# The first expert of a routed feed-forward moved from plain fp32 matmuls to split fp32r matmuls, with the order of the program remade

## The chip, the cores and the metric

The kernel runs on one core of a Trainium2 chip. The metric is the device time of one execution in microseconds (us). The engines of the core are PE (TensorE, matmuls; PEld is its weight load), DVE (VectorE), ACT (ScalarE), POOL (GpSimd) and SP (SyncE, which here issues nearly all transfers). Each engine takes its instructions in the order in which the program lists them.

## The reference

Attention with four sink positions and a window of 128 comes first; its output, as 3072 tokens of 512 numbers, goes through a layer of 8 experts, of which each token uses one:

```python
scores = np.where(is_sink | in_window, q @ k.T / sqrt(64), -1e9)   # 4 x 8 heads, 768 x 768
a = softmax(scores)
x = (a @ v) as 3072 x 512
e_idx = np.argmax(x @ w_gate, axis=1)
for e in range(8):
    mask = e_idx == e
    h = np.maximum(x[mask] @ w1[e], 0.0)            # 512 -> 1024
    out[mask] = gate_w * eom * (h @ w2[e])          # 1024 -> 512
```

Everything is float32.

## The kernel before

**Attention** runs over 16 pairs of heads (4 batches of 4 pairs). For a pair, PE computes the scores in three steps (L1256) into tiles named d, DVE masks them and takes row maxima (L1270, L1272; the "fold"), ACT takes exponentials (L1277, two for each of 6 blocks of 128 rows) into e, PE transposes them (L1305), ACT copies them out (L1308), POOL masks two copies f and g (L384), PE multiplies by v (L1373) and adds the sinks (L1396), ACT copies the result to ot (L1402, with a small tick before the second half, L1387), PE computes the gate logits (L1412) and transposes the output (L1445), and DVE scales both (lw, L1420; x, L1448) before SP stores x to a table xd in device memory.

**Routing** follows after each batch, as some thirty small DVE instructions and three matmul steps (L524 to L622): which expert each token takes, its place in the expert's list (pos, tokpos, ohrow), and after the second and third batch which experts have most tokens (u, gt, rank, perm, order).

**Experts.** A slot is a piece of one expert: up to 6 units of 64 tokens with the whole 4 MB of that expert's weights. Four slots of 256 tokens, numbers 0 to 3, are early: two for the experts ranked after the second batch, two after the third. Thirteen more follow when all tokens are routed, over sizes of 384, 256, 128 and 64 tokens. For a slot, POOL gathers the tokens (xg, L899), PE transposes them (L964), ACT and DVE write them as high and low parts xh and xl (L967, L969); eight tiles of 512 KB are loaded to raw (L936), ACT writes each as its high part (L939, names ending in h, such as wa0h) and DVE the rest as its low part (L943, names ending in l). The products go as three matmuls, high by high, low by high and high by low (L1083 for the first layer, L1122 for the second); the first layer's result is split into hh and hl as well (L1000, L1003).

**The plain slot.** `PLAIN = 1` makes slot 0 an exception. Its eight weight tiles are loaded as plain float32, without conversion, into the space of four pairs wa0 to wa3 (the h and l tile of a pair hold one weight tile each), and it multiplies in plain fp32 (L1064 and L1122), where each matmul stands as two records in the trace. Its result needs no low part (hh alone, L1070).

**Buffers.** Raw has four tiles. Weights have four pairs wa from the start, three pairs wb which take the space of q, k and e once attention has read those for the last time (`close_q`), and six pairs wc which take the rest of the attention's space (`close_a`). The low parts hl and xl lie in a pool mp that also opens with `close_q`.

**Order.** The order of all instructions is set by a planner (`Plan.order`) from a model of costs, from offsets for each kind of step (`AT`), and from times pinned to single steps (`PIN`). The `SOFT` slack lets the plain slot's matmuls give way to attention. Loads before the end of attention are paced by small writes of POOL to their target (`touch`, L1143), each behind a mask step of a certain pair.

Of the kernel before, what the change touches and what calls it, by code (L numbers as in the profile page):

```python
# [51 lines left out]
SOFT = 10509  # L52
SLOT0, STEP, PLAIN, FSTEP = 186561, 20000, 1, 800
# [4 lines left out]
    "load": -31160, "v": -31097, "vs": -28707, "s0": -1104, "s1": 2946, "s2": 3862, "fold": 6328, "exp": -295,  # L58
    "tr0": 5205, "tr1": 8027, "tr2": 9541, "trc": 0, "mask": -3518, "guard": 127, "pack": 3756, "skT": 10500,
# [297 lines left out]
def moe_kernel(tc, qT, kx, vx, vs, wgo, w1, w2, nsink, window, out):  # L357
# [7 lines left out]
    with ctx:  # L365
        const = ctx.enter_context(tc.tile_pool(name="const", bufs=1))
        rt = ctx.enter_context(tc.tile_pool(name="rt", bufs=1))
# [538 lines left out]
        def weights(p, k, which, reg, whole, at, plain=False):  # L906
# [3 lines left out]
            for i in range(4):  # L910
# [19 lines left out]
                if k == PLAIN and not which:  # L930
                    touch([raw], lambda raw=raw: p.get(raw), paced[11 + (8 + i) // 3, (8 + i) % 3], at + i)
# [796 lines left out]
```

## Time and profile before

| | |
|---|---|
| time, median of 3 runs | 514.47 us (514.12 to 519.23) |
| the profiled execution | 515.66 us |
| its span in the trace | 514.0 us |
| PE busy | 480.6 us (94%) |
| DVE, ACT, POOL busy | 326.8, 281.6, 159.3 us |
| moved by DMA | 112.35 MB, mean 219 GB/s |

The profiled execution is one run beside the three; 1.7 us of its time lie outside its span. Busy time of PE is an upper view of its work, because the ends of its matmuls are modelled and overlap.

### The profile page before, as it was taken

The numbers are of one execution on the slowest core, as the hardware profiler recorded it, in microseconds if no ns is written. First come the engines' busy times: TensorE is split into PE (matmuls) and PEld (weight loads), VectorE is DVE, ScalarE is ACT, GpSimd is POOL, SyncE is SP. The second block draws the span as 40 slices with busy tenths as digits, with TensorE's granted clock in tenths as the row PEclk, the third lists the DMA queues.
The fourth block names the chain that finished last, engine by engine and source line by source line (L and its number), as shares of the span: only waits on it lengthen the run. The fifth ranks groups of instructions, "written<-read, shape, count | busy, mean of one in ns | idle before, by whom it ended". The sixth has DMA issues, their size and how long they took to land.

```text
span 514.0 us, 14382 instructions
## 1 busy us (share of the span) xinstructions
PE 480.6 (94%) x5625; PEld 390.4 (76%) x5625; DVE 326.8 (64%) x702; ACT 281.6 (55%) x774; POOL 159.3 (31%) x284
## 2 busy tenths in 40 slices
PE   7899988979899979999999999999999999999993
PEld 3677867757678866688898988978975977986861
DVE  5575866888686667559998963237525688267710
ACT  3878885657597534454556334246525667257510
POOL 5536543647653530204082113022203210101011
PEclk9999999979999999999999999999999999999998
DMA  6674664536695293856498753819679978888930
GB/s 203 214 224 111 220 217 126 169 100 195 200 346 178 87 297 94 282 176 204 153 307 319 233 205 96 294 46 339 199 275 332 331 270 284 301 297 320 352 121 29
DMA packets 61295, 112.35 MB, mean 219 GB/s; under 512 B 8027, under 2 KB 27617, under 8 KB 61218
## 3 DMA queue, kind: packets, MB, share of 16 engines
q1 hardware_dynamic: 56578, 97.06, 56.8%
q0 software_dynamic: 4352, 13.87, 7.5%
q8 instruction: 47, 0.77, 0.6%
q10 hardware_dynamic: 288, 0.41, 0.3%
q14 instruction: 30, 0.25, 0.2%
HBM read 98.14 MB, written 13.31 MB: 217 GB/s over the span
## 4 chain that ended last, share of the span: by engine, by line
PE 62%; DVE 13%; DMA 8%; ACT 6%; issue 6%; POOL 1%; another core or an unknown queue 1%; SPq 1%; POOLq 0%; DVEq 0%; ACTq 0%
PE d L1122 21%; PE d L1083 15%; DMA raw<-in_w_dram 5%; PE d L1373 5%; PE d L1256 4%; PE d L1096 3%; PE d L1064 3%; PE tp L1305 2%; ACT e L1277 2%; DVE nmx L1272 2%; PE tp L964 2%; PE tp L1445 2%; DVE d L1270 2%; PE d L1412 2%; PE d L1030 1%
## 5 line engine op out<-in xcount | busy, mean ns | idle before, releaser
L1277 ACT ACTIVATE e<-d,nmx 128x132 f32<-128x132 f32 x192 | 68.8, 369 | 1.4
L982 POOL DMA_INDIRECT out_dram<-y,idx x20 | 21.2, 1058 | 136.8 <-ACT y L979 107.8
L1000 ACT ACTIVATE hh<-d 128x512 fp32r<-128x512 f32 (+1 forms) x32 | 20.7, 649 | 58.4 <-PE d L1083 56.6
L1256 PE MATMUL d<-k,q 64*64 64x196 f32 (+3 forms) x1088 | 44.2, 283 | 6.8 <-DVE lw L1420 2.0
L1256 PEld LDWEIGHTS d<-k,q 64*64 64x64 f32 x1088 | 36.8, 134 | 15.1 <-issue 6.1
L1003 DVE SCALAR_TENSOR_TENSOR hl<-d,hh 128x512 fp32r<-128x512 f32 (+1 forms) x32 | 24.0, 753 | 34.6 <-ACT hh L1000 34.3
L899 POOL DMA_INDIRECT xg<-xd,idx x20 | 24.5, 1224 | 67.3 <-PE tp L964 44.3
L1373 PE MATMUL d<-f,v 64*64 64x64 f32 (+1 forms) x768 | 41.3, 252 | 2.0 <-ACT e L1277 1.2
L1373 PE MATMUL d<-g,v 64*64 64x128 f32 (+1 forms) x640 | 38.9, 253 | 3.8 <-ACT tick L1387 2.3
L384 POOL TENSOR_SCALAR_AFFINE_SELECT g<-f 128x512 f32<-128x512 f32 (+1 forms) x48 | 27.7, 577 | 43.7 <-ACT f L1308 41.7
L1277 ACT ACTIVATION_READ_ACCUMULATOR e<-d,nmx 128x1 f32 x192 | 39.1, 203 | 0.0
L1373 PEld LDWEIGHTS d<-f,v 64*64 64x64 f32 x768 | 34.1, 135 | 5.9 <-issue 2.5
L1270 DVE COPY_PREDICATED d<-maskf,d 128x512 f32<-128x512 int32 (+1 forms) x48 | 29.0, 604 | 14.0 <-PE d L1256 8.9
L1272 DVE TENSOR_REDUCE nmx<-d 128x4 f32<-128x528 f32 x48 | 33.9, 707 | 1.7
L979 ACT ACTIVATE y<-d,sc 128x512 f32<-128x512 f32 (+1 forms) x28 | 17.5, 656 | 30.6 <-PE d L1122 21.4
L1373 PEld LDWEIGHTS d<-g,v 64*64 64x64 f32 x640 | 29.8, 134 | 5.6 <-ACT tick L1387 3.1
L1305 PE MATMUL tp<-ident,e 128*128 128x128 f32 x192 | 30.3, 285 | 2.4 <-DVE x L1448 1.3
L1308 ACT COPY f<-tp 128x512 f32<-128x512 f32 x48 | 27.5, 586 | 6.6 <-PE tp L1305 6.4
L1305 PEld LDWEIGHTS tp<-ident,e 128*128 128x128 f32 x192 | 21.3, 143 | 10.4 <-DVE x L1448 2.3
L384 POOL TENSOR_SCALAR_AFFINE_SELECT f<-f 128x512 f32<-128x512 f32 (+1 forms) x48 | 27.0, 563 | 3.3
L982 POOL DMA_INDIRECT out_dram<-y,idx_e x8 | 11.8, 1480 | 51.4 <-ACT y L979 49.9
L1284 ACT ACTIVATE nmx<-nmx 128x4 f32<-128x4 f32 x48 | 10.0, 209 | 26.9 <-DVE nmx L1272 26.6
(481 smaller groups left out, 1447.8 us busy)
## 6 DMA issues: line engine op xcount, KB each, us to landing
raw<-in_w_dram SPq DMA_DIRECT2D x96, 512.0 KB
v<-in_vx_dram SPq DMA_DIRECT2D x8, 768.0 KB
xd<-x SPq DMA_DIRECT2D x16, 384.0 KB
k<-in_kx_dram SPq DMA_DIRECT2D x15, 396.0 KB
q<-in_qT_dram SPq DMA_DIRECT2D x15, 384.0 KB
wa1h<-in_w_dram SPq DMA_DIRECT2D x3, 512.0 KB
wa1l<-in_w_dram SPq DMA_DIRECT2D x3, 512.0 KB
wa2h<-in_w_dram SPq DMA_DIRECT2D x3, 512.0 KB
```

What stands on the lines that cost most here:

```text
L384: nc.gpsimd.affine_select(out=ap, in_=ap if src is None else src, pattern=pattern, compare_op=op, fill=fill, base=base, channel_multiplier=cm)
L899: nc.gpsimd.indirect_dma_start(out=p.get(key), out_offset=None, in_=xd[0:n + 1, :], in_offset=bass.IndirectOffsetOnAxis(ap=ids(), axis=0))
L982: nc.gpsimd.indirect_dma_start(out=where, out_offset=bass.IndirectOffsetOnAxis(ap=ids(), axis=0), in_=p.get(yk)[:, 0:m], in_offset=None, b ...
L1083: nc.tensor.matmul(out=p.get(ps)[:, j, 0:cols], lhsT=a, rhs=p.get(x)[:, d, 0:cols], start=d == 0 and i == 0, stop=d == ND - 1 and i == 2)
L1122: nc.tensor.matmul(out=p.get(ys[s][0])[:, ys[s][1], :], lhsT=h[a][:, s * P:(s + 1) * P], rhs=w[b_], start=f == 0 and i == 0, stop=f == NF ...
L1256: nc.tensor.matmul(out=to, lhsT=get(q)[r, qs], rhs=get(k)[r, c:c + n], start=True, stop=True)
L1270: nc.vector.copy_predicated(out=y[:, :, D + 4:3 * D + 4].rearrange("p n (u c) -> p n u c", u=2), mask=bc(maski[:, 1, 4:CW].rearrange("p (u ...
L1272: nc.vector.tensor_reduce(out=top(), in_=z[:, :, :, D:3 * D + 4], axis=AX.X, op=ALU.max, negate=True)
L1277: nc.scalar.activation(out=get(e)[:, t, a, :], in_=by_step()[:, a, i, D:3 * D + 4], func=AF.Exp, bias=get(nmx)[:, a, t:t + 1], scale=SCALE ...
L1305: nc.tensor.transpose(out=get(tp)[:, i, :], in_=get(e)[:, 2 * j + i // 2, i % 2, 4:CW], identity=ident)
L1308: nc.scalar.copy(out=get(f)[:, two].rearrange("p t a r -> p (t a) r"), in_=get(tp))
L1373: nc.tensor.matmul(out=o, lhsT=get(v)[rows_, kt, p % 2 * P + a * D:p % 2 * P + (a + 1) * D], rhs=get((f, g)[src == "g"])[rows_, kt, a, c0: ...
```

## The change

`PLAIN` becomes 0. Slot 0 then runs like slots 1 to 3: its weights go through raw and through a high and a low part, its products are three fp32r matmuls in place of one plain fp32 matmul, and its hidden values get a low part. Since this starts while attention still holds q, k and e, the low parts hl (4 tiles) and xl move from the pool mp, which is gone, to the pool m0, which is open from the start. The four pairs wa now hold half of slot 0's weights, and the other half waits in raw for `close_q`. All numbers that set the order (`AT`, `PIN`, `SLOT0`, `SOFT`) are new; `SOFT` no longer applies to any step.

```diff
-SOFT = 10509
-SLOT0, STEP, PLAIN, FSTEP = 186561, 20000, 1, 800
+SOFT = 9763
+SLOT0, STEP, PLAIN, FSTEP = 184276, 20000, 0, 800
...
-    "load": -31160, "v": -31097, "vs": -28707, "s0": -1104, "s1": 2946, "s2": 3862, "fold": 6328, "exp": -295,
+    "load": -23906, "v": -17027, "vs": -32208, "s0": -211, "s1": 21366, "s2": 9120, "fold": 12815, "exp": -634,
...
-                    touch([raw], lambda raw=raw: p.get(raw), paced[11 + (8 + i) // 3, (8 + i) % 3], at + i)
+                    touch([raw], lambda raw=raw: p.get(raw), paced[11 + (8 * PLAIN + i) // 3, (8 * PLAIN + i) % 3], at + i)
...
-                             ("hh", 4, "m0")):
+                             ("hh", 4, "m0"), ("hl", 4, "m0"), ("xl", 1, "m0")):
...
-            opened["mp"] = mctx.enter_context(tc.tile_pool(name="mp", bufs=1, side="right", reuse_waits="tile"))
...
-        for fam, n, pool, gate, n0 in (("hl", 4, "mp", xq, 0), ("xl", 1, "mp", xq, 0), ("hr", 3, "mc", xa, 0), ("xf", 1, "mc", xa, 0),
+        for fam, n, pool, gate, n0 in (("hr", 3, "mc", xa, 0), ("xf", 1, "mc", xa, 0),
```

In the new program every line after the tables stands 15 lines further down: the fold is L1285 and L1287, the casts L954, the gate L1427, and so on.

The first place is DVE in the routing of the second batch, up to the first lw that stands behind it; d is a score tile, and L1270/L1272 are folds. Before:

```order
L671 TENSOR_TENSOR perm<-rank,io_95 128x16
L672 TENSOR_TENSOR pe<-perm,io_95 128x16
L584 SCALAR_TENSOR_TENSOR den<-z,den 128x6
L585 RECIPROCAL denw<-den 128x96
L675 TENSOR_REDUCE od<-pe 128x2
L676 CAST order_i<-od 128x2
L1420 TENSOR_TENSOR lw_2240<-d_118,rs_1729 128x192
```

The same place on DVE in the new order:

```order
L681 TENSOR_REDUCE rank<-gt 128x8
L1285 COPY_PREDICATED d_119<-maskf,d_119 128x4x128
L1287 TENSOR_REDUCE nmx_2159<-d_119 128x2x2
L686 TENSOR_TENSOR perm<-rank,io_95 128x16
L687 TENSOR_TENSOR pe<-perm,io_95 128x16
L608 CAST jf<-ji 128x12
L609 TENSOR_TENSOR ohj<-jf,ioj 128x96
L690 TENSOR_REDUCE od<-pe 128x2
L691 CAST order_i<-od 128x2
L615 TENSOR_TENSOR ohrow<-io_97,jf 128x768
L1285 COPY_PREDICATED d_118<-maskf,d_118 128x4x128
L1287 TENSOR_REDUCE nmx_2240<-d_118 128x2x2
```

Before, nineteen rows (174 to 192 of DVE, nearly all of routing) stand between two folds; now folds stand after the rank step and after ohrow, with twelve rows ahead of the first and seven between the two.

The second place is ACT among the exponentials of the thirteenth and fourteenth pair (L1277 before, L1292 after). Before:

```order
L1277 ACTIVATE e_2592,rs_2593<-d_120,nmx_2534 128x132 x4
L1387 COPY tick_2785<-d_118 128x1
L1284 ACTIVATE nmx_2754<-nmx_2754 128x2x2
L1277 ACTIVATE e_2800,rs_2801<-d_119,nmx_2754 128x132 x4
L1308 COPY f_2724<-tp_2788 128x512
```

The same place on ACT in the new order:

```order
L1292 ACTIVATE e_2609,rs_2610<-d_118,nmx_2563 128x132 x4
L1402 COPY tick_2778<-d_119 128x1
L954 CAST wa1h<-raw_2627 128x1024
L1299 ACTIVATE nmx_2749<-nmx_2749 128x2x2
L954 CAST wa2h<-raw_2654 128x1024
L1323 COPY f_2702<-tp_2789 128x512
L1292 ACTIVATE e_2831,rs_2832<-d_120,nmx_2749 128x132 x2
L1417 COPY ot_2853<-d_119 128x2x3x128
L1292 ACTIVATE e_2831,rs_2832<-d_120,nmx_2749 128x132 x2
L1323 COPY f_2702<-tp_2855 128x512
L954 CAST wa3h<-raw_2768 128x1024
```

Three of the four casts of slot 0's first-layer weights now stand between exponentials (the first stands 14 rows ahead of the second); before, ACT's first cast came after attention's last exponential.

The third place is PE at the end of attention, from the sinks of the last pair on. Before, a first-layer step of slot 1 (L1083, 24 matmuls) stood between the sinks and the gate, and slot 0's second layer began behind the gate:

```order
L1396 MATMUL d_119<-psk_194,vst_195 64x384 x4
L1083 MATMUL d_118<-xh_3657,wb0h 128x256
...
L1445 MATMUL tp_3765<-ident,ot_3759 128x128 x4
L1445 MATMUL tp_3770<-ident,ot_3759 128x128 x2
L1412 MATMUL d_119<-wgt,ot_3759 64x16 x24
L1122 MATMUL d_120<-wa2h,hh_3453 128x512 x4
```

The same place on PE in the new order:

```order
L1411 MATMUL d_118<-psk_194,vst_195 64x384 x4
L1427 MATMUL d_118<-wgt,ot_3795 64x16 x24
L1460 MATMUL tp_3829<-ident,ot_3795 128x128 x4
L1460 MATMUL tp_3837<-ident,ot_3795 128x128 x2
L1137 MATMUL d_119<-wb0h,hh_3583 128x512
L1137 MATMUL d_119<-wb0l,hh_3583 128x512
```

The gate now stands right behind the sinks of its pair, and slot 0's second layer reads its weights from wb0 in high and low parts.

## Rows read from the trace of the kernel before

**Rows 1.** The page: busy time and share of the engines; PE clock in 40 slices.
```profile
PE 480.6 (94%) x5625; PEld 390.4 (76%) x5625; DVE 326.8 (64%) x702; ACT 281.6 (55%) x774; POOL 159.3 (31%) x284
PEclk9999999979999999999999999999999999999998
```

**Rows 2.** The chain that ended last, 155 to 262 us: start, length, piece.
```profile
162.92 1.73 PE d L1064 x8
...
170.11 5.18 PE d L1064 x24
...
196.60 7.06 PE d L1122 x16
203.67 2.88 PE d L1083 x24
206.55 6.87 PE d L1122 x16
213.41 2.88 PE d L1083 x24
216.29 8.16 PE d L1122 x36
```

**Rows 3.** Instructions of L1064: durations min/median/max in ns, first and last start.
```profile
L1064 PE MATMUL d<-xh,wa0h x16: 379/379/483, 162.8 to 181.5; 128*128 128x256 f32 x16
```

**Rows 4.** Groups of instructions by line on ACT and DVE.
```profile
L939 ACT CAST wa0h<-raw 128x1024 fp32r<-128x1024 f32 x11 | 11.5, 1048 | 9.6 <-PE d L1096 8.5 <-DMA raw<-in_w_dram 0.6 <-issue 0.3
...
L1003 DVE SCALAR_TENSOR_TENSOR hl<-d,hh 128x512 fp32r<-128x512 f32 (+1 forms) x32 | 24.0, 753 | 34.6 <-ACT hh L1000 34.3
...
L969 DVE TENSOR_TENSOR xl<-tp,xh 128x512 fp32r<-128x512 f32 x22 | 14.7, 683 | 8.9 <-ACT xh L967 8.9
L943 DVE TENSOR_TENSOR wa0l<-raw,wa0h 128x1024 fp32r<-128x1024 f32 x11 | 13.4, 1218 | 1.9 <-ACT wa0h L939 1.7
```

**Rows 5.** Busy time in windows of 20 us (PE, PEld, DVE, ACT, POOL), clock, DMA share, GB/s.
```profile
140.00:160.00 20.00, 19.19 (x509) 15.79 (x509) 16.48 (x39) 15.99 (x73) 8.80 (x27) 1.00 1.00 322
160.00:180.00 20.00, 20.00 (x231) 17.31 (x227) 13.03 (x34) 11.75 (x33) 11.21 (x20) 1.00 0.27 88
180.00:200.00 20.00, 17.12 (x288) 12.90 (x279) 12.38 (x40) 6.22 (x14) 4.50 (x4) 1.00 0.69 227
200.00:220.00 20.00, 20.00 (x91) 13.52 (x90) 12.48 (x13) 11.73 (x14) 3.07 (x2) 1.00 0.71 223
220.00:240.00 20.00, 19.90 (x142) 18.13 (x141) 15.78 (x35) 10.88 (x15) 4.19 (x4) 1.00 0.64 199
```

**Rows 6.** Windows of 2 us around the routing of the second batch.
```profile
104.00:106.00 2.00, 1.09 (x20) 0.71 (x20) 1.86 (x10) 1.41 (x7) 0.76 (x1) 1.00 0.08 21
106.00:108.00 2.00, 0.41 (x7) 0.42 (x10) 1.90 (x8) 0.00 (x0) 0.39 (x2) 0.90 0.00 0
108.00:110.00 2.00, 1.85 (x26) 1.30 (x18) 1.93 (x5) 0.02 (x1) 1.22 (x2) 0.50 0.23 25
110.00:112.00 2.00, 1.40 (x7) 1.21 (x8) 1.97 (x4) 1.90 (x10) 0.00 (x0) 0.50 0.86 276
112.00:114.00 2.00, 2.00 (x29) 1.47 (x29) 1.09 (x6) 1.31 (x6) 0.81 (x2) 0.50 0.98 318
114.00:116.00 2.00, 2.00 (x58) 1.72 (x52) 1.00 (x3) 1.35 (x6) 1.70 (x2) 0.89 0.01 2
sum 12.00, PE 8.75 PEld 6.83 DVE 9.74 ACT 5.99 POOL 4.89; mean PE 1.46 PEld 1.14 DVE 1.62 ACT 1.00 POOL 0.81
```

**Rows 7.** PE's timeline there: start, length, what, and the idle time before it.
```profile
107.59 1.65 PE L1256 MATMUL d<-k,q 64*64 64x128 f32 x24 [2.03 <-DVE lw L1420]
```

**Rows 8.** PE's waits over the whole run, the longest.
```profile
PE d L1373 <- ACT tick L1387: 2.3, 2, 2.1
```

**Rows 9.** Window of 226 to 250 us; then PE's timeline in it.
```profile
226.00:250.00 24.00, 22.56 (x164) 20.22 (x164) 22.53 (x69) 13.01 (x19) 5.48 (x5) 1.00 0.56 173
...
248.63 0.66 PE L964 MATMUL tp<-ident,xg 128*128 128x128 f32 x4 [1.01 <-DVE tab L622]
```

**Rows 10.** The chain, 376 to 400 us: a load of raw behind four others.
```profile
379.67 0.38 SPq L925
...
383.90 9.27 DMA raw<-in_w_dram
```

More of the change, by code (lines that the diff above doesn't have):

```diff
@@ L51 @@
 PAIR, RAT = 9500, 17500
-SOFT = 10509
-SLOT0, STEP, PLAIN, FSTEP = 186561, 20000, 1, 800
+SOFT = 9763
+SLOT0, STEP, PLAIN, FSTEP = 184276, 20000, 0, 800
 AT = {
-    "load": -31160, "v": -31097, "vs": -28707, "s0": -1104, "s1": 2946, "s2": 3862, "fold": 6328, "exp": -295,
-    "tr0": 5205, "tr1": 8027, "tr2": 9541, "trc": 0, "mask": -3518, "guard": 127, "pack": 3756, "skT": 10500,
[3 rows of a table removed]
+    "load": -23906, "v": -17027, "vs": -32208, "s0": -211, "s1": 21366, "s2": 9120, "fold": 12815, "exp": -634,
+    "tr0": 2554, "tr1": 8112, "tr2": 11988, "trc": -937, "mask": 20086, "guard": -5960, "pack": 2664, "skT": 10478,
[3 rows of a table added]
 }
 PIN = {
[59 rows of a table removed]
[74 rows of a table added]
 }
@@ L1672, in moe_kernel @@
                 now = tensors(Now())
-                for fam, n, pool, n0 in (("sc", 8, "mx", 0), ("xg", 2, "mc", 4), ("xh", 1, "mx", 0), ("xl", 1, "mp", 0), ("hh", 4, "m0", 0), ("hl", 4, "mp", 0),
+                for fam, n, pool, n0 in (("sc", 8, "mx", 0), ("xg", 2, "mc", 4), ("xh", 1, "mx", 0), ("xl", 1, "m0", 0), ("hh", 4, "m0", 0), ("hl", 4, "m0", 0),
                                          ("hr", 3, "mc", 0), ("y", 4, "mc", 0), ("raw", RAW, "stg", 0)):
```

139 rows, old and new, of tables (AT, PIN) are left out of this document.

## The prediction

> **What bounds the kernel now.** I read first the busy shares of the page [rows 1]: PE is busy 94% of the span, the next engine 64%, so only PE's work and PE's few gaps can pay. I then read the chain that ended last around the place where slot 0 runs [rows 2]. The reader is to see that from 162.9 us on nearly every piece of the chain is a PE piece, so that a matmul saved there moves all that follows. Windows of 20 us show the same from the other side [rows 5]: from 140 to 240 us PE is busy 96.2 of 100 us. DVE and ACT have room there, and DMA (share 0.27 to 1.00) is not full except before 160 us. Last I looked where PE loses time inside attention. The windows of 2 us from 104 to 116 us [rows 6] are the worst stretch: PE is busy 8.75 of 12 us, and its granted clock is at its lower level, 1.2 GHz, for the three windows from 108 to 114 us, after PE had been busy for only 1.50 of the 4 us before. DVE is busy 7.66 of the first 8 us, with routing, and PE waits 2.03 us for an lw that stands behind it [rows 7].
>
> **First layer of slot 0.** In plain fp32, 24 records last 5.18 us unbroken and 8 last 1.73 us [rows 2], 0.216 us each. There are 64 (16 of each of four weight tiles, [rows 3] being one), so 13.8 us. Split in three, the step of 24 matmuls of the same shape takes 2.88 us in slot 1 [rows 2]; slot 0 needs four, 11.5 us. This term is -2.3 us.
>
> **Second layer.** The plain one is two pieces of 16 records, 7.06 and 6.87 us [rows 2], 13.9 us. Split, 36 matmuls take 8.16 us, 0.227 us each, and 48 are needed: 10.9 us. This term is -3.0 us. Both together are -5.3 us, and both lie on the chain, on PE, whose work is behind them until the end.
>
> By the rows the split form costs 22.4 of the plain form's 27.7 us, a ratio of 0.81 [rows 2]. The Trainium skill, on the page "FP8 and Floating Point Precision", section "TensorE Precision Notes", says that true FP32 takes four passes through the array (high and low parts each by each); three of those four products are kept, so by it the ratio would be 0.75 and the saving 6.9 us, not 5.3. The rows speak against the full quarter, since they hold the rate of both forms.
>
> **What slot 0 adds on ACT and DVE.** Eight casts at 1.05 us (8.4 us of ACT), eight low parts at 1.22 us, four hl at 0.75 us and two xl at 0.68 us (14.1 us of DVE) [rows 4]. Half of the weights, four casts and four low parts, fall in attention's last third, among the exponentials and folds. Their cover is the free time of ACT and DVE there: 4.0 and 3.5 of 20 us at 140 to 160 us, 8.3 and 7.0 at 160 to 180 us [rows 5]. The price is nothing if all lies in that free time and 9.1 us (4 times 1.05 + 1.22) if all of it stops PE. PE idles only 0.8 us in 140 to 160 us although DVE and ACT are then at 80%, which is nearest to the low end: I take +1.5 us. The other half comes after attention's last read of e. There the four hl and four low parts are 7.9 us of DVE, against 7.6 free us at 180 to 200 us and 7.5 at 200 to 220 us [rows 5]: nothing, with the first rival for the case that the cover fails. POOL's touches fall from 12 to 4, on an engine that is not waited for there: nothing.
>
> **Loads.** Slot 0's first four tiles pass through raw as the direct ones did through wa; its other four keep raw full until wb opens, so slot 1's loads start some 2 MB later. After 180 us the DMA share is 0.64 to 0.71 [rows 5] and PE still has slot 0's second layer to do (10.9 us) before it needs slot 1; at the 227 GB/s moved in 180 to 200 us, 2 MB are 9 us. Nothing, and at most the difference to no cover, 9 us, which I leave to the range.
>
> **The end of attention.** The gate of the last pair now stands right behind its sinks, with no first-layer step between. Before, that place had a wait of 2.1 us for a tick [rows 8], the longest of its kind. The new wait is the copy to ot, and what ACT does before it. I put one for the other: 0, between -2 and +2.
>
> **The order inside attention.** The stretch of rows 6 lost 3.25 us idle and, at half clock, half of the 5.25 us busy in 108 to 114 us and a little at 114 to 116 us, 2.8 us: 6.1 us in all. In the new order the routing of the second batch is laid out with folds after rank and after ohrow, so that scores reach ACT during it, and an lw stands ahead of its second half. That removes the cause as the rows show it (PE without scores for some 4 us) if the rest of the new order keeps PE as busy. All other steps of attention have moved too, and the trace cannot price them: a gain of 6.1 us at one end, and at the other the same stretch and one more like it, +6.1. I take half of the gain, -3.0, since the cause is visibly thinned but not gone.
>
> **The sum.** -5.3 + 1.5 - 3.0 = -6.8 us. From the profiled execution's own 515.66 us that gives 508.9; that execution lies 1.2 us above the median of the three runs, 514.47, against which I forecast: 507.7 us. A change under about 1% (5.1 us, so from 509.3 to 519.6) cannot be told from none here.
>
> **Rivals.**
> The saving is given back after attention (chance 0.14). From 226 to 250 us DVE is busy 22.5 of 24 us and PE waits 1.01 us for the routing table at its end [rows 9], so DVE nearly bounds that stretch already. With half an expert's weights handled later, four low parts (4.9 us) would be pushed into it if the free time of 200 to 240 us were not used. For it: DVE's queue is fixed, and low parts wait for ACT's casts. Against it: 11.7 us are free in those 40 us [rows 5]. Time: 507.7 + 4.9 = 512.6 us.
>
> ACT stops at casts whose load has not landed (chance 0.09); this one ends slower. The casts of wa1, wa2 and wa3 stand among the exponentials of pairs 13 and 14, and until a tile has landed nothing behind its cast runs: no exponentials, so no transposes, no PE work. A load behind four others, issued from 379.7 us on, took 9.27 us from issue to landing [rows 10], and at 140 to 160 us DMA is already full [rows 5]. The Trainium skill, page "TensorE: Matmul & The Clock Gate", section "Architectural detail: the array is 16× 32×32, not 1× 128×128", says that ScalarE and VectorE run their queues strictly in order; that PE waits for an lw while DVE works off the routing ahead of it [rows 7] agrees. Against the rival: two pairs of exponentials and copies lie between issue and cast. Two such waits in full are 18.5 us; two thirds of that, 12 us, give 519.7 us. It decides against the change from 6.8 us of waiting on.
>
> The lower clock stays, or moves elsewhere in attention (0.18): only the matmuls pay, 514.47 - 5.3 + 1.5 = 510.7 us.
>
> The whole stretch is freed and the casts are hidden (0.13): 514.47 - 5.3 - 6.1 = 503.1 us.
>
> Three passes for four in full (0.03): 6.9 in place of 5.3 saved, 507.7 - 1.6 = 506.1 us, by the rule above.
>
> **How the numbers follow.** The forecast has 0.43, with a range of its own from 504 to 511 us. Faster by over 1%: 0.37 of the forecast, the freed stretch, the passes and a quarter of the staying clock, 0.57. Slower by over 1%: most of the stopped casts, 0.07. Within 1%: 0.36. The range for 8 in 10 runs from 501 us (the freed stretch with 2 us for the end of attention) to 516.5 us (the saving given back, with the 4 us of the loads beyond it); it leaves out the stopped casts and the outer ends.
>
> **What would show it.** In the new trace the records of L1064's successor are gone, and slot 0 shows 96 first-layer and 48 second-layer fp32r matmuls at 0.12 and 0.23 us. If the order's term is right, PE's clock row has no slice under 9 between the start and the end and no wait for lw above 1 us. If the casts stop ACT, its longest waits name raw. If DVE gives the saving back, PE's waits around the last batch's routing name tab, hl or low parts for over 1.3 us. The forecast is wrong if attention ends later than the 196.6 us at which the last gate ended before, less the 5.2 us that slot 0's first layer (2.3) and the moved step of slot 1 (2.9) take out of it.

## The result and the profile after

The changed kernel takes 508.48 us in the median (507.72 to 510.98, four runs); the kernel before, on the same chip, 514.30 us. The ratio is 0.986, with an interval of 0.982 to 0.990: faster by 5.0 to 9.4 us. The forecast was 507.7 us. The profiled execution took 507.72 us, with a span of 506.0.

The page of the changed kernel, with the rows that answer to [rows 1]:
```profile
PE 474.9 (94%) x5673; PEld 395.2 (78%) x5673; DVE 335.8 (66%) x716; ACT 290.1 (57%) x782; POOL 161.6 (32%) x276
PEclk9899999999998989999999999999999999999997
```
PE is busy 5.7 us less than before while its span is 8.0 us shorter: part of the gain is not matmul work. The clock row has no 7 in its ninth slice any more, but an 8 in the second, the thirteenth and the fifteenth.

The chain of the changed kernel through slots 0 and 1, which answers to [rows 2] (L1098 is the split first layer, L1137 the split second):
```profile
165.83 2.91 PE d L1098 x24
...
170.55 3.03 PE d L1098 x24
...
174.46 5.66 PE d L1098 x48
...
192.28 1.40 PE d L1137 x6
...
194.34 4.13 PE d L1137 x18
198.47 2.83 PE d L1098 x24
201.29 5.45 PE d L1137 x24
```
Slot 0's first layer is 2.91 + 3.03 + 5.66 = 11.6 us, its second 1.40 + 4.13 + 5.45 = 11.0 us. The reader should also see that a step of slot 1 has moved. In the chain of the kernel before, these pieces, which [rows 2] leaves out, stand there too:
```profile
165.24 1.83 PE d L1064 x8
...
167.95 1.73 PE d L1064 x8
...
177.55 1.92 PE d L1064 x8
...
181.27 1.93 PE d L1064 x8
...
192.06 3.07 PE d L1083 x24
```
The step of slot 1 (L1083) stood ahead of the last gate; now it comes behind it (198.47), which by itself ends attention some 2.9 us sooner without any gain at the end. With the four other pieces, the plain first layer took 1.73 + 1.83 + 1.73 + 5.18 + 1.92 + 1.93 = 14.3 us.

Windows of the changed kernel, 20 us each as in [rows 5], and of 2 us as in [rows 6]:
```profile
120.00:140.00 20.00, 17.14 (x448) 14.61 (x447) 17.63 (x33) 16.27 (x60) 12.36 (x24) 1.00 0.87 285
140.00:160.00 20.00, 17.64 (x375) 14.22 (x373) 18.19 (x59) 14.65 (x62) 13.78 (x24) 0.91 0.43 125
...
106.00:108.00 2.00, 1.96 (x43) 1.58 (x41) 1.43 (x3) 1.82 (x9) 0.82 (x2) 1.00 0.24 74
112.00:114.00 2.00, 1.15 (x57) 0.95 (x51) 1.97 (x5) 2.00 (x9) 1.93 (x3) 1.00 0.66 190
sum 12.00, PE 10.72 PEld 8.85 DVE 10.91 ACT 8.77 POOL 6.02; mean PE 1.79 PEld 1.47 DVE 1.82 ACT 1.46 POOL 1.00
```
Between 104 and 116 us PE is now busy 10.72 us in place of 8.75, all at the upper clock. From 140 to 160 us it is the other way about: DVE is at 18.2 of 20 us and PE is busy 1.6 us less than in [rows 5].

PE's waits in the changed kernel, in answer to [rows 7 to 9]:
```profile
PE d L1427 <- ACT ot L1417: 2.1, 3, 0.9
PE d L1388 <- ACT tick L1402: 1.1, 2, 0.9
PE tp L979 <- DVE tab L637: 1.1, 1, 1.1
PE d L1271 <- DVE lw L1435: 0.8, 1, 0.8
```
The lw wait fell from 2.03 to 0.8 us, the tick wait from 2.1 to 0.9; the gate waits for ot 0.9 us at most; tab is where it was.

The chain of the changed kernel from 376 to 425 us, the stretch of [rows 10]:
```profile
378.53 2.73 PE d L1137 x12
...
397.83 8.48 PE d L1098 x72
...
410.50 5.49 PE d L1137 x24
```
Before, a load of raw stood on the chain here ([rows 10]); now every piece from 376 to 425 us is PE's. The forecast has no term for this stretch. From here on the experiments decide how much belongs to which part.

### The profile page after: what moved, and what is told of

Read it like the earlier page. It is cut to its first block, busy times and chain, and to the rows that moved or that the text cites. A ratio compares the mean times of both kernels' runs of the same rounds, so it can differ in the third digit from the quotient of the medians.

```text
span 506.0 us, 14497 instructions
## 1 busy us (share of the span) xinstructions
PE 474.9 (94%) x5673; PEld 395.2 (78%) x5673; DVE 335.8 (66%) x716; ACT 290.1 (57%) x782; POOL 161.6 (32%) x276
## 4 chain that ended last, share of the span: by engine, by line
PE 68%; ACT 10%; DVE 9%; issue 5%; DMA 4%; POOL 2%; another core or an unknown queue 0%; SPq 0%; POOLq 0%; ACTq 0%; DVEq 0%
PE d L1137 24%; PE d L1098 20%; ACT e L1292 5%; PE d L1111 4%; PE d L1388 4%; PE d L1271 3%; PE tp L979 2%; PE d L1045 2%; PE tp L1320 2%; DVE nmx L1287 2%; DVE d L1285 1%; PE d L1427 1%; ACT f L1323 1%; PE d L1059 1%; PE tp L1460 1%
## 5 line engine op out<-in xcount | busy, mean ns | idle before, releaser
L1292 ACT ACTIVATE e<-d,nmx 128x132 f32<-128x132 f32 x192 | 69.2, 372 | 1.8
L1015 ACT ACTIVATE hh<-d 128x512 fp32r<-128x512 f32 (+1 forms) x36 | 23.2, 645 | 58.5 <-PE d L1098 47.6
L1018 DVE SCALAR_TENSOR_TENSOR hl<-d,hh 128x512 fp32r<-128x512 f32 (+1 forms) x36 | 26.9, 746 | 37.6 <-ACT hh L1015 31.1
L1271 PE MATMUL d<-k,q 64*64 64x128 f32 (+3 forms) x1088 | 44.6, 284 | 4.3 <-DMA k<-in_kx_dram 2.2
L1388 PE MATMUL d<-f,v 64*64 64x64 f32 (+1 forms) x768 | 43.8, 257 | 2.4 <-issue 1.4
L399 POOL TENSOR_SCALAR_AFFINE_SELECT g<-f 128x512 f32<-128x512 f32 (+1 forms) x48 | 29.0, 604 | 49.5 <-ACT f L1323 49.0
L1388 PE MATMUL d<-g,v 64*64 64x64 f32 (+1 forms) x640 | 39.7, 258 | 3.7 <-issue 2.5
L1292 ACT ACTIVATION_READ_ACCUMULATOR e<-d,nmx 128x1 f32 x192 | 39.4, 205 | 0.0
L1285 DVE COPY_PREDICATED d<-maskf,d 128x512 f32<-128x512 int32 (+1 forms) x48 | 28.9, 603 | 12.0 <-PE d L1271 11.0
L1287 DVE TENSOR_REDUCE nmx<-d 128x4 f32<-128x528 f32 x48 | 34.0, 707 | 1.7
L984 DVE TENSOR_TENSOR xl<-tp,xh 128x512 fp32r<-128x512 f32 x24 | 16.3, 684 | 9.6 <-ACT y L994 6.0
```

The source lines that it names most:

```text
L399: nc.gpsimd.affine_select(out=ap, in_=ap if src is None else src, pattern=pattern, compare_op=op, fill=fill, base=base, channel_multiplier=cm)
L1018: nc.vector.scalar_tensor_tensor(out=p.get(hl)[:, :, 0:n], in0=p.get(ps)[:, :, 0:n], scalar=0.0, in1=p.get(hh)[:, :, 0:n].bitcast(F32), op ...
L1271: nc.tensor.matmul(out=to, lhsT=get(q)[r, qs], rhs=get(k)[r, c:c + n], start=True, stop=True)
L1285: nc.vector.copy_predicated(out=y[:, :, D + 4:3 * D + 4].rearrange("p n (u c) -> p n u c", u=2), mask=bc(maski[:, 1, 4:CW].rearrange("p (u ...
L1287: nc.vector.tensor_reduce(out=top(), in_=z[:, :, :, D:3 * D + 4], axis=AX.X, op=ALU.max, negate=True)
L1292: nc.scalar.activation(out=get(e)[:, t, a, :], in_=by_step()[:, a, i, D:3 * D + 4], func=AF.Exp, bias=get(nmx)[:, a, t:t + 1], scale=SCALE ...
```

## The experiments

Chips differ: the median of the kernel before was 512.4 to 517.3 us on the three chips of these runs. So each version is given as a ratio to the kernel before on its own chip, with its interval; 0.001 is 0.5 us.

The experiments are named e1 to e12, as e4 for the kernel before run again.

**Which rows belong to a kernel, and which to one execution (e4, e5, e12).** Both kernels were run again unchanged, so there is no diff.

> The kernel before, unchanged, profiled a second time, to see which of its waits belong to the kernel and which to one execution. If the 2.24 us of idle TensorE between 340 and 488 us are the kernel's own: again about 2.2 us there, in waits for an xf and an xl, and a part of the gain lies in the later slots. If they were that execution's: less than 0.5 us there and a span nearer to 512 us. The half-clock stretch near 108 to 114 us should be there again if the order makes it.

> The changed kernel, unchanged, on the same chip and beside the same runs of the kernel before as the other three. If the first four times stand for it: a ratio of 0.982 to 0.990. The three places with half clock (14 to 19, 151 to 155 and 185 to 189 us) and a TensorE without idle time between 340 and 460 us should come again if the order makes them.

> The changed kernel, unchanged, on the same chip and beside the same runs of the kernel before as the other three, as their measure: a ratio of 0.978 to 0.990 as in its two earlier measurements.

The changed kernel gave 0.982 (0.978 to 0.986) and 0.988 (0.984 to 0.992); with the first 0.986 the mean of the three is 0.985, or -7.6 us. The clock rows of the kernel before again, then of the changed kernel's second and third execution:
```profile
PEclk9999999979999989999999999999999999999997
```
```profile
PEclk9999999999999999999999999999999999999998
```
```profile
PEclk9999989999998987999999999999999999999998
```
The 7 in the ninth slice is there in all five executions with the old order of attention (two of the kernel before, and those of e1, e7 and e8 below) and in none of the nine with the new. But the new order has no fixed slow place of its own: leaving out the last slice, the three executions of one program show three slices under 9, none, and four. The waits between 340 and 480 us, on the other hand, came back in the kernel before, with PE idle 4.56 us in place of 2.24:
```profile
PE tp L964 <- ACT xf L967: 1.2, 1, 1.2
PE d L1096 <- ACT xh L967: 1.0, 1, 1.0
...
340.00:480.00 140.00, 135.44 (x800) 108.99 (x799) 83.53 (x92) 77.34 (x111) 23.88 (x20) 1.00 0.79 278
```
The three executions of the changed kernel have no idle PE there at all. So these waits come back with the old kernel, though their length does not.

**The order from slot 4 on (e6, e7).** The table PIN also changed for the 13 later slots. It was exchanged for them alone, both ways. The diff is the first differing line of e6, of some twenty-five; a step of the changed kernel has a number 10 higher than the same step of the kernel before:

```diff
-    1308: 238888, 1311: 253446, 1320: 262945, 1324: 246947, 1327: 254871, 1328: 269575, 1329: 263445, 1330: 257566,
+    1308: 238888, 1311: 253446, 1320: 262945, 1324: 247947, 1327: 247946, 1328: 269575, 1329: 263445, 1330: 253871,
...
```

> The changed kernel with the table's numbers from slot 4 on taken from the kernel before; attention, routing and slots 0 to 3 as changed. Theory: the 2.2 to 4.6 us of idle TensorE between 340 and 488 us that all three traces with the old numbers there have, and no trace with the new ones has, belong to the order of casts and loads of the later slots, so that this gives back 2 to 4 us: a ratio of about 0.993 where the changed kernel has 0.987. Rival: they come from slot 0's own loads, which go straight into wa in plain form and through raw in split form, so that the later slots' numbers do nothing: the same ratio as the changed kernel, within 0.002.

> The kernel before with the table's numbers from slot 4 on taken from the changed kernel; everything ahead of slot 4 as it was. Theory (the later order makes its gain by itself): 2 to 4 us under the kernel before, a ratio of 0.992 to 0.996, without waits for xf and xl between 380 and 460 us. Rival (slot 0's loads): a ratio of 1.00, with those waits still there.

The changed kernel with the old later numbers gave 0.986 (0.982 to 0.990), beside 0.982 for the changed kernel on the same chip: 2.0 us given back. The kernel before with the new ones gave 0.995 (0.992 to 0.998): 2.4 us gained with nothing else changed. The intervals of the first two overlap, that of e7 lies clear of 1. PE's time from 340 to 480 us, first of the kernel before with new later numbers, then of the changed kernel with old ones:
```profile
340.00:480.00 140.00, 140.00 (x823) 113.37 (x821) 84.55 (x94) 76.76 (x112) 22.82 (x19) 1.00 0.81 286
```
```profile
340.00:480.00 140.00, 139.05 (x823) 113.18 (x823) 86.89 (x99) 78.91 (x116) 21.04 (x19) 1.00 0.86 306
```
The idle time goes and comes with these numbers: all four executions with the old ones have some (0.95 to 4.56 us: the kernel before twice, e2 and e6); of the ten with the new ones nine have none and one 0.24 us (e3). With it come the loads on the chain, here again in the changed kernel with old later numbers:
```profile
402.57 0.94 ACT wb1h L952
...
403.54 1.24 DVE wb1l L956
...
406.37 5.72 DMA raw<-in_w_dram
...
412.11 1.06 ACT wc1h L952
```
A cast and a low part free a raw tile; its next load takes 5.7 us and has landed 7.3 us after the low part's end, and the next cast waits for that. This part of the change is worth 2.0 to 2.4 us (e7 by itself: 0.9 to 3.9). The rival (slot 0's loads) would have kept the waits in the plain kernel; they went.

**The order of attention and routing (e2, e8, e1).** Three versions: the plain slot 0 in the new order (e2), the split slot 0 with the old numbers (e8), and the split slot 0 with each step of attention held to the old order (e1). The hold, in e1 and e2, is a list for each engine that the planner must follow (an extract):

```diff
+        follows = {}
+        for xs in KEEP.values():
+            for a, b in zip(xs, xs[1:]):
+                follows[a] = b
+                missing[b] += 1
```

> Slot 0 in plain fp32 as before, with every step of attention and of the routing in the order of the changed kernel; slot 0's plain steps stand where the split ones stand. As predicted (order -3.0 by itself): 514.3 - 3.0 = 511.3 us, and no half-clock stretch near 108 to 114 us. Rival: the new order gives back at 144 to 156 us and 182 to 190 us what it frees at 104 to 116 us, 514 us, no change. Second rival: the new order was made for the split form and is worse with the plain one, 516 us or more.

> The changed kernel with the numbers that set the order of attention and routing taken from the kernel before, and the planner left to put slot 0's casts and steps among them: unlike the first experiment it may move steps of attention against each other. As predicted, by the sum without the order's term and with 1.5 us for the casts, 2 us above the changed kernel: a ratio of 0.991. If the old order has no room for the casts, however they are placed, as the first experiment says: 1.00 or more, with attention's last gate after 196 us.

> Slot 0 split in high and low parts, with every step of attention and of the routing in the order of the kernel before; slot 0's own transposes and first-layer steps stand where the plain ones stood, the four casts and low parts of its first weights are put in where the planner finds room, and its second-layer weights and slot 1's follow as pools allow. As predicted (matmuls -5.3, conversions +1.5, order -3.0): 514.3 - 5.3 + 1.5 = 510.5 us, about 2 us above the changed kernel's 508.5, with the half-clock stretch near 108 to 114 us still there. Rival, after the new trace, in which attention ends only where the matmuls alone put it: the order gave nothing and the conversions cost nothing, 514.3 - 5.3 = 509.0 us, no difference from the changed kernel that can be told. Second rival, the new order is what hides the casts: without it they stop the exponentials, 512 us or more.

The plain slot 0 in the new order (AT and PIN below 1053 and the list of the changed kernel, the rest of the kernel before) gave 0.996 (0.992 to 0.999), -2.2 us. The split slot 0 with AT and PIN below 1053 of the kernel before, without a list, gave 0.9895 (0.985 to 0.995); the changed kernel on that chip has 0.982, so the new numbers are worth 3.8 us there. The two put the order's term between -2.2 and -3.8 us, both with wide intervals: that of e2 alone reaches from -0.4 to -4.0 us, and that of e8 overlaps that of the changed kernel beside it (0.978 to 0.986).

How the order gains is less plain than that it does. The mean granted clock of all executions is 0.9860 in e8 and 0.9937 in the changed kernel on that chip. That difference alone would be some 3.9 us, as an estimate: 0.0077 less in the mean is 1.5% of the 505 us spent at 1.2 in place of 2.4 GHz, 7.8 us, of which half is lost. But in e2 the mean clock is 0.987, as in the kernel before on its chip, and the 2.2 us are gained all the same. And on the chip of e12 the changed kernel has a lower mean clock than the kernel before (0.982 and 0.984).

The split by itself can be read from e8 and e7. They share the chip, the old order of attention and the new numbers from slot 4 on, and differ in the form of slot 0 and the numbers of slots 0 to 3: 0.9895 to 0.995, -3.0 us, again with intervals that overlap. The sum has -5.3 + 1.5 = -3.8 for this.

Held to the old order step by step, the split slot 0 gave 1.006 (1.002 to 1.010), slower than before. Two of its windows, and two of PE's waits from 100 to 203 us, for x and for ticks:
```profile
140.00:160.00 20.00, 16.37 (x394) 12.60 (x394) 17.03 (x38) 16.14 (x70) 10.44 (x19) 1.00 0.81 268
180.00:200.00 20.00, 13.19 (x286) 10.25 (x283) 15.76 (x33) 11.03 (x18) 10.13 (x8) 1.00 0.65 213
...
PE tp L1041 <- DVE x L1525: 2.1, 1, 2.1
PE d L1450 <- ACT tick L1464: 2.6, 2, 1.6
```
PE idles 27.4 us in attention in place of 19.8, 6.8 of it from 180 to 200 us, where x and ticks stand behind casts and low parts of slots 0 and 1. Since the same numbers without the list lost nothing of the kind, this run does not price the old order as such. What it shows is that the casts and low parts did not fit into the old sequence as it was held, with no step of attention giving way: the second rival of that run.

**What the conversions cost (e3, e9, e11, e10).** On the changed kernel, whose order on every engine stays as it is: casts and low parts of slot 0's first weights twice (e3); the low parts left out, with the high part in their place in the third product, so that this output is not the layer's (e9); the casts alone twice (e11); the casts moved to GpSimd (e10). Extracts of the diffs of e3, e9 and e10:

```diff
-                def hi(raw=raw, key=key):
-                    nc.scalar.copy(out=p.get(key)[0], in_=p.get(raw))
+                def hi(raw=raw, key=key, n=TWICE if k == 0 and not which else 1):
+                    for _ in range(n):
+                        nc.scalar.copy(out=p.get(key)[0], in_=p.get(raw))
...
-                    tt(out=l, in0=p.get(raw), in1=h.bitcast(F32), op=ALU.subtract)
+                    if k or which:
+                        tt(out=l, in0=p.get(raw), in1=h.bitcast(F32), op=ALU.subtract)
...
-                def hi(raw=raw, key=key):
-                    nc.scalar.copy(out=p.get(key)[0], in_=p.get(raw))
+                def hi(raw=raw, key=key, make=nc.gpsimd.tensor_copy if k == 0 and not which else nc.scalar.copy):
+                    make(out=p.get(key)[0], in_=p.get(raw))
```

> The changed kernel, with the four casts and four low parts of slot 0's first-layer weights each made twice: 4.2 us more on ScalarE and 4.9 us more on VectorE among the steps of attention from about 118 to 140 us. As predicted (1.5 us for one such dose): 508.5 + 1.5 = 510.0 us. If their cover holds: 508.5 us. If all of it stops TensorE: 508.5 + 9.1 = 517.6 us.

> The changed kernel without the four low parts of slot 0's first-layer weights (4.9 us of VectorE at about 122 to 142 us); the third product takes the high part in their place, so the matmuls are as many and as long, and that part of the output is computed from other numbers. As predicted (1.5 us for all eight conversions): about 0.8 us under the changed kernel on the same chip. After the doubled dose, which cost about half of its own length: if that came from VectorE, 2.5 us under; if it came from ScalarE, no difference.

> The changed kernel with only the four casts made twice (4.2 us more of ScalarE; the low parts once). With both doubled the loss was about 5 us. If ScalarE's strict row of exponentials carries it: 3 us or more over the changed kernel on the same chip. If VectorE's row carries it: less than 1 us over.

> The changed kernel with the four casts of slot 0's first-layer weights made by GpSimd instead of ScalarE, at the same place in the program: 4.2 us less among the exponentials, four more instructions among GpSimd's masks of the folds. If ScalarE's time is what the conversions cost: 2 us under the changed kernel on the same chip. As predicted (0.7 us of the 1.5 for ScalarE's part): 0.7 us under. Rival: the folds wait for masks that stand behind the casts, 2 us or more over it.

Both twice: 0.995 (0.991 to 0.999), which is 5 us above the changed kernel's mean of 0.985; 9.1 us were added. The other three ran beside the changed kernel's third measurement, 511.85 us in the median (ratio 0.988). Without the low parts: 508.74 us and 0.983 (0.979 to 0.986), 2.6 us less by the ratios and 3.1 by the medians, for 4.9 us of DVE. Casts alone twice: 512.86 us and 0.990 (0.986 to 0.994), 1.0 to 1.2 us more, for 4.2 us of ACT. Casts on GpSimd: 510.93 us and 0.988 (0.985 to 0.992), no difference that can be told; a cast there is as long as on ACT (1.05 us):
```profile
L954 POOL CAST wa1h<-raw 128x1024 fp32r<-128x1024 f32 x1 | 1.0, 1038 | 0.0
```
So the low parts on DVE carry most of the price, and the casts on ACT little, if anything: 1 us is within the noise. The intervals of the runs with and without low parts overlap too (0.984 to 0.992 and 0.979 to 0.986), so 2.6 us is a size with an uncertainty of some 2 us, but the doubled dose points the same way: 5 us less the 1 us of the casts leaves 4 for as much again on DVE. Only slot 0's first weights were tried; its other conversions have no run. At 120 to 140 us DVE is busy 17.63 of 20 us in the changed kernel; with the low parts left out that window reads:
```profile
120.00:140.00 20.00, 16.62 (x443) 14.32 (x444) 13.17 (x32) 15.65 (x60) 8.86 (x21) 1.00 0.91 304
```
DVE falls to 13.17 us. So without the low parts 6.8 of these 20 us are free on DVE, more than the 4.9 us that they take, and they cost some 2.6 us nevertheless.

## Why the prediction came out right, step by step

**First and second layer (-2.3 and -3.0): right, the first a little small.** The second went from 13.9 to 11.0 us, -2.9. The first went to 11.6 us; the prediction put its plain form at 13.8 us from its two best pieces, where all six add up to 14.3, so it is -2.7. Split to plain is then 22.6 to 28.2, 0.80. The Trainium skill's count of passes ("FP8 and Floating Point Precision", "TensorE Precision Notes": four in true FP32, of which three are kept) would make it 0.75, as an estimate that takes every pass to be as long as a split matmul; the trace decides against the full quarter, since a plain matmul took as long as 3.7 split ones, not four.

**Conversions (+1.5): too small by about half.** They cost some 3 us, nearly all of it through the low parts. The step that failed is the price read from free time: the prediction took DVE's free 3.5 and 7.0 us in the windows of 140 to 180 us of the kernel before as a cover for most of the work. In the changed kernel the low parts stand from 121.9 to 138.3 us, between folds and rows of the second batch's routing. There was free time there too, 6.8 us in e9 for 4.9 us of low parts, and it did not cover them. Free time summed over 20 us does not say whether the step that waits behind a low part is one that PE waits for.

**Loads (0) and the end of attention (0 ± 2): right, and the sign for them too fine.** No wait of ACT for raw up to the last gate is longer than 0.3 us in the three executions of the changed kernel; tick and ot make PE wait 0.9 us at most. Attention ends at 191.48 us, against the limit of 191.4 beyond which the forecast was to be wrong: by this sign the forecast just failed in that execution, where the matmuls and the moved step explain all of the earlier end, and the order's gain and the conversions' cost cancel. In the other two executions attention ends at 184.6 and 195.7 us, so one execution cannot decide this sign.

**The order inside attention (-3.0): the size is right, the picture only half.** It measures -2.2 and -3.8 us. PE's empty stretch at 104 to 116 us and the half clock behind it are gone in every execution of the new order, as forecast, and in the three of the changed kernel no lw holds PE for more than 0.8 us. But over the whole of attention, from 4.6 us to the last gate, the first traces show no less idle time and no higher clock; first the kernel before, then the changed one:
```profile
4.60:196.60 192.00, 172.22 (x3871) 139.07 (x3870) 134.28 (x330) 130.89 (x555) 94.93 (x213) 0.98 0.61 191
```
```profile
4.60:191.48 186.88, 167.25 (x3867) 137.82 (x3867) 139.24 (x338) 137.51 (x561) 97.89 (x205) 0.97 0.59 185
```
PE idles 19.8 us in the one and 19.6 in the other. The lower clock shows elsewhere: the sign that no slice is under 9 failed in eight of the nine executions of the new order, and in seven of them the slices are between 140 and 205 us. Three of the five with the old order (e4, e7 and e8) have one there too, beside their ninth, so the new order did not make that place slow by itself. The rival that the lower clock moves (510.7 us) describes the first trace of attention better than the forecast does.

**What the sum left out.** The order from slot 4 on is worth -2.0 to -2.4 us. The prediction quoted the very rows that show the loss ([rows 10], a load on the chain at 383.9 us), used them to price a rival, and called nearly every piece of the chain PE's. The rest of the chain from 376 us on was not read.

With the measured sizes the sum is -5.6 + 3 - 3 - 2.2 = -7.8 us, and the three measurements of the changed kernel have -7.6 in the mean. That the forecast's -6.8 came so near is in part luck: the missing gain of the later slots (-2.2) and the missing cost of the conversions (+1.5) nearly cancel. Of the other rivals, DVE did not give the saving back (PE idles 1.57 us from the last gate to 300 us, 1.44 before), and no cast stopped ACT for a load.

What stays open: where in attention the order gains, and which of its steps the low parts delay. The traces are single executions whose clocks differ by more than the price, so only the times tell it. A part of the low parts' price may be paid in clock: without them the mean granted clock of the six executions is 0.9857, with them 0.9820, by the reckoning of e8 an estimated 1.9 of the 2.6 us.

## What to carry to other kernels

Do not price added work by an engine's free time in a window: here 4.9 us of low parts cost some 2.6 us where 6.8 of 20 us were free. Leave the work out, or do it twice, and measure. Follow the chain to its end before saying what bounds the kernel: a DMA piece between long runs of matmuls is a gain that someone may take. And exchange tables of an order by stage: a run each way tells what a whole-kernel time cannot.

## What the runs showed of the hardware

The lower clock is only in part a property of the program. One slow place, at 104 to 116 us, came with the old order in all five executions; others come and go while the program stays the same. These are attention's windows, from 4.6 us to the last gate, of the second and of the third execution of the changed kernel, on two chips:
```profile
4.60:184.60 180.00, 163.39 (x3867) 133.66 (x3866) 137.69 (x337) 136.68 (x560) 98.21 (x205) 1.00 0.59 189
```
```profile
4.60:195.70 191.10, 171.48 (x3866) 139.88 (x3865) 139.29 (x338) 137.46 (x561) 97.76 (x205) 0.96 0.58 184
```
The same matmuls keep PE busy 163.4 us at a mean clock of 1.00, and 171.5 at 0.96: 8.1 us, more than the whole change. A mean of 0.96 is 8% of 191 us, 15 us, at 1.2 GHz, which costs half of that, 7.6. Idle time adds 3.0 us (16.6 and 19.6). It is not the chip alone: the six executions of e12 on one chip had mean clocks from 0.975 to 0.987. The Trainium skill ("TensorE: Matmul & The Clock Gate", "Part 1: The HAM clock gate (the "warmup" mystery)") says that at its start one and the same kernel runs a different number of matmuls at the lower clock from run to run. The traces show the like in mid-kernel. The Trainium skill, in the same section, puts the loss at the start at under 1% of a typical span; the loss here, most of it behind the start, is 7.6 of 511.8 us, 1.5%.
